# Values and the next pair's scores in one piece, and a new order of the last accumulators, in an attention and GLU kernel

## The chip, the cores and the metric

One of the eight NeuronCores of a Trainium2 chip runs the whole kernel. Its engines work from queues of their own and wait for each other through semaphores: TensorE (PE; its loads of weights are a row PEld), VectorE (DVE), ScalarE (ACT), GpSimd (POOL) and the queue engine SyncE (SP). The metric is device time in microseconds (us) of one execution.

## What is computed

Attention over 8 batches, 8 heads, 576 positions and 64 channels, with two kinds of sparse mask, and on its output a gated layer whose three products are with matrices of 512 x 1536, 512 x 1536 and 1536 x 512.

```python
def _attn_ref(q, k, v):
    scores = scale * np.matmul(q, k.transpose(0, 1, 3, 2))
    mask_local = (rel >= 0) & (rel < stride)              # stride = 32; heads 0 to 3
    mask_strided = (rel >= 0) & (pos[None, :] % stride == pos[:, None] % stride)   # heads 4 to 7
    ...
    attn = np.exp(scores - np.max(scores, axis=-1, keepdims=True))
    attn = attn / (np.sum(attn, axis=-1, keepdims=True) + 1e-09)
    return np.matmul(attn, v)

def _moe_ref(x, w_gate, w_val, w_out):     # x: 4608 tokens x 512
    gate = 1.0 / (1.0 + np.exp(-(x @ w_gate)))
    val = x @ w_val
    return gate * val @ w_out
```

## The kernel before

The gated layer goes over nine blocks of 512 tokens: block k holds the first 512 positions of batch k, and block 8 the 64 left over of all eight batches. A block has twelve chunks f of 128 hidden channels. Operands are kept as a high and a low part, and each product is made of three: high by high, low by high, high by low. So a chunk has three blocks of twelve TensorE products of 128 x 128 by 512: the gates g (`glu_gate`), the values v (`glu_val`), and the out-products o of a chunk (`glu_out`) into four accumulators of 128 tokens each. g and v have one PSUM bank each; the accumulators 0 and 1 share a tile of two banks, and 2 and 3 another; the last two banks are one tile "a" for attention.

Between the products stand the elementwise steps of a chunk. ScalarE makes t (tanh of half of g) and e (exp of g); VectorE clears t's sign (L386), multiplies min(e, 1) by v (L410), and by 1 + t (L411); ScalarE rounds it to hh (L402), VectorE makes hl, what is left (L405). t and e have one buffer each, hh and hl three.

Attention for batch k + 1 runs while block k does. A batch has four pairs of heads, local and strided in turn (`pair`), and a pair has these steps: Q and V load q with k, and v; Z clears pads; S makes the scores (small TensorE matmuls, `score`); F adds the mask, takes the maximum and subtracts it (VectorE); E is the exp (ScalarE); N the normalization (VectorE); B transposes the probabilities in 32 x 32 blocks (VectorE, L261); X weighs the values (small matmuls, `weigh`); H, L and R split the result into the high and low x of the coming block (xh on ScalarE, xl on VectorE), and keep the 64 positions left over (xr). Local scores use TensorE in tiles of 64 x 32, strided scores and all values in tiles of 64 x 64 (54 rows of it for strided values).

TensorE's order is written by hand: `block` walks the three slots of each chunk (gates, values, out-products of the chunk before), and calls the generator `attention` behind the slots 0 and 7 of every nine. Its first call of a pair records Q to B, its second X to R. So scores stand behind a chunk's gates, and the values of the same pair two chunks on, behind that chunk's values. The other engines' orders come from a scheduler. Batches 0 and 1 and block 0 are done in an earlier stage (`ORDER`) that the change leaves alone.

At a block's end `give_out` copies its four accumulators (ScalarE the even ones, VectorE the odd) and stores each through SP's queue. In block 8 the out-products of the last two chunks are done together, accumulator by accumulator; each is copied as soon as its products are done, the last one in two halves, one by each copying engine; and each copy is stored in two pieces of 64 rows, one for each batch. A read of a tile by a copy holds back later products into that tile.

Of the kernel before, what the change touches and what calls it, by code (L numbers as in the profile page):

```python
# [9 lines left out]
F32 = mybir.dt.float32  # L10
# [4 lines left out]
ALU = mybir.AluOpType  # L15
AX = mybir.AxisListType

B, H, S, D = 8, 8, 576, 64
DM, DF = 512, 1536
NT = B * S  # L20
P = 128
# [16 lines left out]
TB = 512  # L38
REST = S - TB
MAIN = TB // STRIDE  # L40
NTT = TB // P
NB = NT // TB
NC = DM // P
NF = DF // P
BANK = 512
BY_PE = 2
AT = (0, 7)
LATE = NF - 1

BANKS = {  # L50
# [33 lines left out]
def attention_then_glu(ctx, tc, qk_l, qk_s, v_l, v_s, w_all, consts, out):  # L84
    nc = tc.nc
    pool = ctx.enter_context(tc.tile_pool(name="keep", bufs=1))
    work = ctx.enter_context(tc.tile_pool(name="work", bufs=1))

    cst = pool.tile([P, SL * KL + GS + P], F32, name="cst")
    mask_l = cst[:, : SL * KL].rearrange("p (j n) -> p j n", j=1)  # L90
    mask_s = cst[:, SL * KL : SL * KL + GS].rearrange("p (t k) -> p t k", t=1)
# [3 lines left out]
    def left_over(b):  # L95

        if b == 0:
            xr[0] = pool.tile([P, NC, 2 * REST], F32, name="xr0")
        if b == 2:
            xr[2] = stage("raw1", "xr2").bitcast(F32).rearrange("p (c n) -> p c n", c=NC)  # L100
        if b == 6:
            xr[6] = stage("h0", "xr6").bitcast(F32).rearrange("p (c n) -> p c n", c=NC)
# [3 lines left out]
    def x_tiles(b):  # L106
        xs[b] = [(odd if b % 2 else work).tile([P, NC, TB], F32R, tag=t, name=f"{t}{b}") for t in ("xh", "xl")]
# [56 lines left out]
    def pair(b, step, space):  # L164

        local, p = step % 2 == 0, step // 2
        c = p if local else 2 + p
        ns, kk = (SL, KL) if local else (SS, GS)
# [26 lines left out]

        todo = {}

        def score(sc):
            qk = tiles["qk"]

            m = LB if local else QB
            for n in range(ns * (P // m)):
                s, g = divmod(n, P // m)
                q = n % (NBL if local else NG)
                for j in range(2):
                    d = slice(j * D, (j + 1) * D)
                    q0, k0 = (q * LB, S + q * LB) if local else (q * GS, SK + q * GS)
                    nc.tensor.matmul(  # L208
                        sc[g * m : (g + 1) * m, j * BANK + s * kk : j * BANK + (s + 1) * kk],
                        qk[d, q0 : q0 + m],  # L210
                        qk[d, k0 : k0 + kk],
                        start=True,
                        stop=True,
                    )
            todo["soft"] = sc.rearrange("p (j n) -> p j n", j=2)[:, :, : ns * kk]

        def soft():
            sc = todo["soft"]
            prob, row, by_row = rows()
            if local:  # L220
                to = tiles["sb"][:, : 2 * ns * kk].rearrange("p (j n) -> p j n", j=2)
                nc.vector.tensor_tensor(to, sc, mask_l.broadcast_to([P, 2, ns * kk]), op=ALU.add)
            else:
                for j in range(2):
                    to, sv = prob[:, j * ns : (j + 1) * ns], sc[:, j].rearrange("p (t k) -> p t k", k=kk)
                    nc.vector.tensor_tensor(to, sv, mask_s.broadcast_to([P, ns, kk]), op=ALU.add)
            nc.vector.tensor_reduce(row, prob, axis=AX.X, op=ALU.max)
            nc.vector.tensor_tensor(prob, prob, by_row, op=ALU.subtract)  # L228

# [96 lines left out]
        def keep_rest():  # L326
# [3 lines left out]

        return dict(
            Q=load_qk, V=load_v, Z=room, S=score, F=soft, E=expo, N=norm, T=turn, B=turn_blocks, P=spread, X=weigh, H=split_high,
            L=split_low, R=keep_rest,
        )

    def bank(tag, name):
        return ps.tile([P, 2 * BANK], F32, tag=tag, name=name)

    def attention(b):

        x_tiles(b)
        left_over(b)
        for step in range(4):
            do = pair(b, step, work)
            do["Q"](), do["V"](), do["Z"]()
            do["S"](bank("a", f"s{b}_{step}"))
            do["F"](), do["E"](), do["N"](), do["B"]()
            yield
            do["X"](bank("a", f"x{b}_{step}"))
            do["H"](), do["L"](), do["R"]()  # L350
            yield

    def split_rest():
# [17 lines left out]
    def glu_gate(k, f, g=None):  # L371
        if g is None:
            g = ps.tile([P, BANK], F32, tag="g", name=f"g{k}_{f}")
            products(g, k, f, 0)
        e = work.tile([P, TB], F32, tag="e", name=f"e{k}_{f}")
        hs[k, f] = e
        if k == 0:
            nc.scalar.activation(e, g, AF.Sigmoid)
            return
        t = work.tile([P, TB], F32, tag="t", name=f"t{k}_{f}")  # L380
        hs[k, f] = (t, e)

        nc.scalar.activation(t, g, AF.Tanh, scale=0.5)  # L383
        nc.scalar.activation(e, g, AF.Exp)  # L384
        ti = t.bitcast(I32)
        nc.vector.tensor_scalar(ti, ti, 0x7FFFFFFF, None, op0=ALU.bitwise_and)  # L386

    def glu_val(k, f, v=None):
        if v is None:
            v = ps.tile([P, BANK], F32, tag="v", name=f"v{k}_{f}")  # L390
            products(v, k, f, 1)
        if k == 0:
            e, t = hs[k, f], work.tile([P, TB], F32, tag="t", name=f"t{k}_{f}")
        else:
            t, e = hs[k, f]
        hh = work.tile([P, TB], F32R, tag="hh", name=f"hh{k}_{f}", bufs=3)
        hl = work.tile([P, TB], F32R, tag="hl", name=f"hl{k}_{f}", bufs=3)
        hs[k, f] = (hh, hl)
        half = 1.0 if k == 0 else 0.5

        def high():
            nc.scalar.activation(hh, t, AF.Copy, scale=half)  # L402

        def low():
            nc.vector.scalar_tensor_tensor(hl, t, half, hh.bitcast(F32), op0=ALU.mult, op1=ALU.subtract)  # L405

        if k == 0:
            nc.vector.tensor_tensor(t, e, v, op=ALU.mult)
            return high, low
        nc.vector.scalar_tensor_tensor(e, e, 1.0, v, op0=ALU.min, op1=ALU.mult)  # L410
        nc.vector.scalar_tensor_tensor(t, t, 1.0, e, op0=ALU.add, op1=ALU.mult)  # L411
        high(), low()
# [14 lines left out]
    def give_out(k, i, cut=slice(0, DM), by=None):  # L427

        tag = ("ost", "l0", "t", "e")[i if k == B else i % 2]
        if (k, i) not in given:  # L430
            given[k, i] = (odd if tag == "ost" else work).tile([P, DM], F32, tag=tag, name=f"ob{k}_{i}")
        ob, o = given[k, i], acc[k][i]
        if by is None:
            by = (nc.scalar.copy, nc.vector.tensor_copy)[i % 2]
        by(ob[:, cut], o[:, cut])  # L435
        if k < B:
            nc.sync.dma_start(out[k * S + i * P : k * S + (i + 1) * P, cut], ob[:, cut])
        else:
            for n in range(P // REST):
                at = (i * P // REST + n) * S + TB  # L440
                nc.sync.dma_start(out[at : at + REST, cut], ob[n * REST : (n + 1) * REST, cut])

    given = {}

    def glu_out(k, *fs):

        if fs[0] == 0:
            two = [bank(f"o{n}", f"o{k}_{n}") for n in range(NTT // 2)]
            acc[k] = [two[i // 2][:, i % 2 * BANK : (i % 2 + 1) * BANK] for i in range(NTT)]
        for i in range(NTT):  # L450
            for f in fs:
                out_products(k, f, i)
            if k == B and fs[-1] == NF - 1 and i < NTT - 1:
                give_out(k, i)
        if fs[-1] < NF - 1:
            return
        if k == B:
            give_out(k, NTT - 1, slice(0, DM // 2), nc.scalar.copy)
            give_out(k, NTT - 1, slice(DM // 2, DM), nc.vector.tensor_copy)
        else:  # L460
            for i in range(NTT):
                give_out(k, i)

    def block(k, f, pend, last):
        for slot in range(3):
            if slot == 0:
                glu_gate(k, f)
            elif slot == 1:
                glu_val(k, f)
            elif (k, f) != (B, NF - 2):  # L470
                glu_out(*last)
            if (3 * f + slot) % 9 in AT:
                next(pend, None)

    for f in range(LATE):
        weight_tiles(f)
# [54 lines left out]
                left_over(1)  # L531

    with tc.manual_schedule(engines={mybir.EngineType.PE}):
        last = (0, NF - 1)
        for k in range(1, NB):
            pend = attention(k + 1) if k + 1 < B else iter(())
            if k == B:
                split_rest()
            for f in range(NF):
                block(k, f, pend, last)  # L540
                last = (k, f) if (k, f) != (B, NF - 2) else last
            for _ in pend:
                pass
        glu_out(B, NF - 2, NF - 1)


# [81 lines left out]
```

## Time and profile before

| | |
|---|---|
| median of three runs | 1006.43 us (1006.33 to 1007.9) |
| the profiled execution, its own time | 1005.89 us |
| its span, first to last instruction | 1004.1 us |
| granted TensorE clock, mean | 0.996 |
| TensorE busy in the 540 us from 180 to 720 | 540.00 us |
| VectorE busy in the same stretch | 337.94 us |

A row of a timeline reads: start and length in us, engine, line of the kernel, operation, output <- inputs, shape, how many in the row, and in brackets how long the engine sat idle before it and what ended that. The chain of waits is followed back from the last instruction; its rows have a start, a length and what the time went to. An end of a matmul in the profile is a model; starts tell how fast TensorE goes.

### The profile page before, as it was taken

The page shows a single profiled execution, that of the slowest core. Times are in us where ns is not written, and L with a number is a line of the kernel's source. Part 1 is how long each engine was busy: PE and PEld are TensorE (multiplying, and loading weights), DVE is VectorE, ACT ScalarE, POOL GpSimd, SP SyncE. Part 2 cuts the span into 40 slices and gives each one's busy share as a digit, 9 for nine tenths or more (in the row PEclk, how much of TensorE's full clock was granted, in tenths as well). Part 3 has the DMA queues.
Part 4 walks back from the last instruction along what each step waited for, and adds up shares of the span by engine and source line. Part 5 has one row for each costly group of instructions (what it writes and reads, how often), then busy time and mean ns, then how long its engine had stood idle before and what let it go on. Part 6 is the DMA issues. An engine that isn't in the chain of part 4 may idle for free.

```text
span 1004.1 us, 18124 instructions
## 1 busy us (share of the span) xinstructions
PE 977.5 (97%) x7840; PEld 795.8 (79%) x7840; DVE 588.8 (59%) x1042; ACT 321.4 (32%) x636; POOL 5.1 (1%) x20
## 2 busy tenths in 40 slices
PE   4998999999999999999999999999999999999997
PEld 4787778888888888888888888888888888888885
DVE  6887776666666566656666666656665633333322
ACT  4787763222222222222322222222222322222221
POOL 0000000000000000000000000000000000000000
PEclk9999999999999999999999999999999999999999
DMA  7666641111211112101211121112110010001001
GB/s 249 225 178 202 207 122 68 41 52 41 90 44 52 41 57 78 40 29 51 84 28 49 41 93 41 52 41 73 61 52 17 1 43 1 0 1 42 1 1 42
DMA packets 20031, 66.02 MB, mean 66 GB/s; under 512 B 2288, under 2 KB 2672, under 8 KB 19952
## 3 DMA queue, kind: packets, MB, share of 16 engines
q1 hardware_dynamic: 18512, 59.28, 18.4%
q10 hardware_dynamic: 1440, 5.59, 1.6%
q8 instruction: 61, 1.00, 0.4%
q14 instruction: 18, 0.15, 0.0%
HBM read 55.42 MB, written 9.44 MB: 65 GB/s over the span
## 4 chain that ended last, share of the span: by engine, by line
PE 90%; DMA 4%; ACT 3%; DVE 2%; issue 0%; SPq 0%; ACTq 0%; DVEq 0%
PE v L369 28%; PE o L419 28%; PE g L369 27%; PE x L289 3%; DMA raw<-in_w_all 3%; PE s L208 3%; ACT high L139 1%; DMA qk<-in_qk_s 1%; ACT low L143 1%; PE t L247 1%; PE gv L369 1%; DVE sb L239 0%; DVE mx L236 0%; ACT sb L232 0%; ACT pt L269 0%
## 5 line engine op out<-in xcount | busy, mean ns | idle before, releaser
L419 PE MATMUL o<-w,hh 128*128 128x512 f32 x864 | 270.5, 394 | 1.4 <-ACT ob L435 1.4
L369 PE MATMUL v<-xh,w 128*128 128x512 f32 x784 | 263.3, 396 | 0.0
L369 PE MATMUL g<-xh,w 128*128 128x512 f32 x784 | 258.6, 390 | 0.0
L419 PEld LDWEIGHTS o<-w,hh 128*128 128x128 f32 x864 | 159.5, 188 | 37.3 <-ACT ob L435 2.2
L369 PEld LDWEIGHTS v<-xh,w 128*128 128x128 f32 x784 | 148.3, 189 | 32.8
L369 PEld LDWEIGHTS g<-xh,w 128*128 128x128 f32 x784 | 147.2, 188 | 30.9
L386 DVE TENSOR_SCALAR t<-t 128x512 int32<-128x512 int32 x96 | 41.0, 427 | 217.4 <-ACT t L383 216.6
L419 PE MATMUL o<-w,hl 128*128 128x512 f32 x432 | 168.4, 390 | 0.0
L369 PE MATMUL v<-xl,w 128*128 128x512 f32 x392 | 154.0, 393 | 0.0
L369 PE MATMUL g<-xl,w 128*128 128x512 f32 x392 | 152.7, 389 | 0.0
L402 ACT ACTIVATE hh<-t 128x512 fp32r<-128x512 f32 x108 | 68.3, 633 | 256.6 <-DVE t L411 256.0
L383 ACT ACTIVATE t<-g 128x512 f32<-128x512 f32 x96 | 57.4, 598 | 262.9 <-PE g L369 262.1
L410 DVE SCALAR_TENSOR_TENSOR e<-e,v 128x512 f32<-128x512 f32 x96 | 65.8, 686 | 91.0 <-PE v L369 91.0
L261 DVE STREAM_TRANSPOSE pt<-sb 32x320 f32<-32x320 f32 (+1 forms) x192 | 102.9, 536 | 3.1
L405 DVE SCALAR_TENSOR_TENSOR hl<-t,hh 128x512 fp32r<-128x512 f32 x108 | 74.6, 691 | 48.5 <-ACT hh L402 48.5
L419 PEld LDWEIGHTS o<-w,hl 128*128 128x128 f32 x432 | 81.1, 188 | 17.5 <-DVE hl L405 0.3
L369 PEld LDWEIGHTS v<-xl,w 128*128 128x128 f32 x392 | 74.3, 189 | 14.5
L369 PEld LDWEIGHTS g<-xl,w 128*128 128x128 f32 x392 | 73.6, 188 | 15.1
L411 DVE SCALAR_TENSOR_TENSOR t<-t,e 128x512 f32<-128x512 f32 x96 | 66.5, 692 | 3.3
L384 ACT ACTIVATE e<-g 128x512 f32<-128x512 f32 x96 | 57.0, 594 | 0.0
L232 ACT ACTIVATE sb<-sb 128x640 f32<-128x640 f32 (+1 forms) x32 | 23.8, 744 | 69.7 <-DVE sb L228 69.7
L289 PEld LDWEIGHTS x<-pt,vv 64*64 64x64 f32 (+1 forms) x1856 | 34.7, 140 | 13.8 <-issue 9.3
(60 smaller groups left out, 656.8 us busy)
## 6 DMA issues: line engine op xcount, KB each, us to landing
raw<-in_w_all SPq DMA_DIRECT2D x36, 512.0 KB, 4.2
qk<-in_qk_s SPq DMA_DIRECT2D x14, 599.0 KB, 4.2
vv<-in_v_l SPq DMA_DIRECT2D x13, 640.0 KB, 3.9
qk<-in_qk_l SPq DMA_DIRECT2D x14, 592.0 KB, 4.0
out<-ob SPq DMA_DIRECT2D x32, 256.0 KB, 2.0
vv<-in_v_s SPq DMA_DIRECT2D x13, 384.0 KB, 3.1
vv<-in_v_l ACTq DMA_DIRECT2D x3, 640.0 KB, 5.2
qk<-in_qk_s ACTq DMA_DIRECT2D x2, 599.0 KB, 4.4
```

The costliest lines, as they stand in the source:

```text
L208: nc.tensor.matmul(sc[g * m : (g + 1) * m, j * BANK + s * kk : j * BANK + (s + 1) * kk], qk[d, q0 : q0 + m], qk[d, k0 : k0 + kk], start=Tr ...
L261: nc.vector.transpose(dst[to : to + LB, :, col : col + LB], src[rows : rows + LB, :, h * LB : (h + 1) * LB])
L289: nc.tensor.matmul(xp[j * D : (j + 1) * D, r * BANK + (u * per + g) * m : r * BANK + (u * per + g + 1) * m], v[rows, (u * per + g) * P + j ...
L369: nc.tensor.matmul(o, w, x, start=first and n == 0, stop=last and n == len(todo) - 1)
L383: nc.scalar.activation(t, g, AF.Tanh, scale=0.5)
L384: nc.scalar.activation(e, g, AF.Exp)
L386: nc.vector.tensor_scalar(ti, ti, 0x7FFFFFFF, None, op0=ALU.bitwise_and)
L402: nc.scalar.activation(hh, t, AF.Copy, scale=half)
L405: nc.vector.scalar_tensor_tensor(hl, t, half, hh.bitcast(F32), op0=ALU.mult, op1=ALU.subtract)
L410: nc.vector.scalar_tensor_tensor(e, e, 1.0, v, op0=ALU.min, op1=ALU.mult)
L411: nc.vector.scalar_tensor_tensor(t, t, 1.0, e, op0=ALU.add, op1=ALU.mult)
L419: nc.tensor.matmul(acc[k][i], h[:, i * P : (i + 1) * P], w, start=f == 0 and n == 0, stop=f == NF - 1 and n == 2,)
```

## The change

A pair's values and the scores of the next pair are recorded by one call of the generator, which now runs over the 24 pairs of batches 2 to 7 without a break. The scores go into the g and v banks, one head in each, in place of tile "a"; only the very first pair's go into "a". Three chunks of a block with attention beside it have the order: gates and values of chunk 3n, out-products; gates and values of 3n + 1; gates and values of 3n + 2, out-products, the joined piece, out-products. Out-products so run one or two chunks behind. The load of a pair's v is recorded behind its F step, that of the next q and k at the end of the call. From block 7 on (no attention beside it) the order of the chunks is that of before.

Everywhere `glu_out` takes the accumulators in the order 0, 2, 1, 3. In block 8 each copy is stored by one DMA over two batches, from ScalarE's queue where ScalarE made the copy.

```diff
-AT = (0, 7)
...
-        def score(sc):
+        def score(*sc):
...
-                        sc[g * m : (g + 1) * m, j * BANK + s * kk : j * BANK + (s + 1) * kk],
+                        sc[j % len(sc)][g * m : (g + 1) * m, j // len(sc) * BANK + s * kk : j // len(sc) * BANK + (s + 1) * kk],
...
-                nc.vector.tensor_tensor(to, sc, mask_l.broadcast_to([P, 2, ns * kk]), op=ALU.add)
+                for j, x in enumerate(sc):
+                    heads = to[:, j : j + x.shape[1]]
+                    nc.vector.tensor_tensor(heads, x, mask_l.broadcast_to([P, x.shape[1], ns * kk]), op=ALU.add)
...
-    def attention(b):
-
-        x_tiles(b)
-        left_over(b)
-        for step in range(4):
-            do = pair(b, step, work)
-            do["Q"](), do["V"](), do["Z"]()
-            do["S"](bank("a", f"s{b}_{step}"))
-            do["F"](), do["E"](), do["N"](), do["B"]()
-            yield
-            do["X"](bank("a", f"x{b}_{step}"))
-            do["H"](), do["L"](), do["R"]()
+    def attention():
+
+        todo = [(b, step) for b in range(BY_PE, B) for step in range(4)]
+        ahead, now = pair(*todo[0], work), None
+        ahead["Q"]()
+        for n, (b, step) in enumerate(todo + [(B, 0)]):
+            if now:
+                of, p = todo[n - 1]
+                if p == 0:
+                    x_tiles(of)
+                    left_over(of)
+                now["X"](bank("a", f"x{of}_{p}"))
+                now["H"](), now["L"](), now["R"]()
+            if b < B:
+                now = ahead
+                now["Z"]()
+                if n == 0:
+                    now["S"](bank("a", f"s{b}_{step}"))
+                else:
+                    now["S"](*(ps.tile([P, BANK], F32, tag=t, name=f"s{b}_{step}_{t}") for t in "gv"))
+                now["F"](), now["V"](), now["E"](), now["N"](), now["B"]()
+                if n + 1 < len(todo):
+                    ahead = pair(*todo[n + 1], work)
+                    ahead["Q"]()
             yield
...
+        queue = nc.scalar if k == B and by == nc.scalar.copy else nc.sync
         if k < B:
-            nc.sync.dma_start(out[k * S + i * P : k * S + (i + 1) * P, cut], ob[:, cut])
+            to = out[k * S + i * P : k * S + (i + 1) * P, cut]
         else:
-            for n in range(P // REST):
-                at = (i * P // REST + n) * S + TB
-                nc.sync.dma_start(out[at : at + REST, cut], ob[n * REST : (n + 1) * REST, cut])
+            to = out.rearrange("(b s) n -> b s n", b=B)[i * P // REST : (i + 1) * P // REST, TB:, cut]
+        queue.dma_start(to, ob[:, cut])
...
-        for i in range(NTT):
+        for i in (0, 2, 1, 3):
...
             for f in range(NF):
-                block(k, f, pend, last)
-                last = (k, f) if (k, f) != (B, NF - 2) else last
-            for _ in pend:
-                pass
+                glu_gate(k, f)
+                glu_val(k, f)
+                last.append((k, f))
+                if k + 1 < B and f % 3 == 2:
+
+                    glu_out(*last.pop(0))
+                    next(pend)
+                    glu_out(*last.pop(0))
+                elif (k + 1 >= B or f % 3 == 0) and (k, f) != (B, NF - 2):
+                    glu_out(*last.pop(0))
+                if (k, f) == (1, 0):
+                    next(pend)
         glu_out(B, NF - 2, NF - 1)
```

Names in the rows below carry batch or block and pair or chunk: x2_1 are the weighted values of batch 2's pair 1, g1_6 the gates of block 1's chunk 6. xN at a row's end counts instructions.

TensorE in block 1, before: the values of pair 1 stand behind the products of chunk 5's values, and the scores of pair 2 behind chunk 6's gates.

```order
L369 MATMUL v1_5_2208<-xl1_570,w5_1_78 128x512
L369 MATMUL v1_5_2208<-xh1_569,w5_1_78 128x512
L289 MATMUL x2_1_2227<-pt2_1_2101,vv2_1_2062 64x54 x22
L419 MATMUL o1_0_1939<-w4_2_76,hh1_4_2172 128x512 x2
L419 MATMUL o1_0_1939<-w4_2_76,hl1_4_2173 128x512
...
L369 MATMUL g1_6_2271<-xl1_570,w6_0_80 128x512
L369 MATMUL g1_6_2271<-xh1_569,w6_0_80 128x512
L208 MATMUL s2_2_2295<-qk2_2_2289 32x64 x40
L369 MATMUL v1_6_2353<-xh1_569,w6_1_81 128x512
L369 MATMUL v1_6_2353<-xl1_570,w6_1_81 128x512
```

After, the same two stand next to each other, between the out-products of chunks 3 and 4:

```order
L433 MATMUL o1_1_1976<-w3_2_73,hh1_3_2126 128x512 x2
L433 MATMUL o1_1_1976<-w3_2_73,hl1_3_2127 128x512
L291 MATMUL x2_1_2230<-pt2_1_2072,vv2_1_2065 64x54 x22
L208 MATMUL s2_2_g_2264<-qk2_2_2081 32x64
L208 MATMUL s2_2_v_2265<-qk2_2_2081 32x64
```

The scores' 40 matmuls keep their order (the first two are shown), and go by turns into the g and the v bank; the products on both sides are out-products.

VectorE in block 2, from the mask add of a strided pair's scores on, before:

```order
L226 TENSOR_TENSOR sb3_3_3520<-s3_3_3523,cst_61 128x6x54 x2
L227 TENSOR_REDUCE mx3_3_3521<-sb3_3_3520 128x12
L228 TENSOR_TENSOR sb3_3_3520<-sb3_3_3520,mx3_3_3521 128x12x54
L410 SCALAR_TENSOR_TENSOR e2_9_3511<-e2_9_3511,v2_9_3566 128x512
L411 SCALAR_TENSOR_TENSOR t2_9_3512<-t2_9_3512,e2_9_3511 128x512
L236 TENSOR_REDUCE mx3_3_3521<-sb3_3_3520 128x12
L405 SCALAR_TENSOR_TENSOR hl2_9_3580<-t2_9_3512,hh2_9_3579 128x512
L237 TENSOR_SCALAR mx3_3_3521<-mx3_3_3521 128x12
L238 RECIPROCAL mx3_3_3521<-mx3_3_3521 128x12
L239 TENSOR_TENSOR sb3_3_3520<-sb3_3_3520,mx3_3_3521 128x12x54
L261 STREAM_TRANSPOSE pt3_3_3557<-sb3_3_3520 32x12x32 x8
L386 TENSOR_SCALAR t2_10_3611<-t2_10_3611 128x512
```

And after, from the same add on:

```order
L228 TENSOR_TENSOR sb3_3_3497<-s3_3_g_3500,cst_61 128x6x54
L228 TENSOR_TENSOR sb3_3_3497<-s3_3_v_3501,cst_61 128x6x54
L229 TENSOR_REDUCE mx3_3_3498<-sb3_3_3497 128x12
L230 TENSOR_TENSOR sb3_3_3497<-sb3_3_3497,mx3_3_3498 128x12x54
L238 TENSOR_REDUCE mx3_3_3498<-sb3_3_3497 128x12
L239 TENSOR_SCALAR mx3_3_3498<-mx3_3_3498 128x12
L240 RECIPROCAL mx3_3_3498<-mx3_3_3498 128x12
L241 TENSOR_TENSOR sb3_3_3497<-sb3_3_3497,mx3_3_3498 128x12x54
L263 STREAM_TRANSPOSE pt3_3_3537<-sb3_3_3497 32x12x32 x8
L400 TENSOR_SCALAR t2_9_3574<-t2_9_3574 128x512
L424 SCALAR_TENSOR_TENSOR e2_9_3573<-e2_9_3573,v2_9_3578 128x512
L425 SCALAR_TENSOR_TENSOR t2_9_3574<-t2_9_3574,e2_9_3573 128x512
```

The add of each head waits for its own bank; the instructions of chunk 9 (t, e, t, hl) stood between the pair's steps and stand behind all of them, the transposes too. At a change of block the copies of accumulators 1 and 3 stood on VectorE ahead of the normalization and behind the transposes; afterwards both stand behind the transposes, ahead of and behind the first chunk's hl.

The last rows of ScalarE and of SP's queue, before, ob8_n being the copy of accumulator n:

```order
L435 COPY ob8_0_8856<-o8_0_8358 128x512
L435 COPY ob8_2_8876<-o8_1_8359 128x512
L435 COPY ob8_3_8886<-o8_1_8359 128x256
L441 DMA out_0<-ob8_0_8856 64x512 x2
L441 DMA out_0<-ob8_1_8866 64x512 x2
L441 DMA out_0<-ob8_2_8876 64x512 x2
L441 DMA out_0<-ob8_3_8886 64x256 x4
```

And after:

```order
L449 COPY ob8_0_8890<-o8_0_8392 128x512
L455 DMA out_0<-ob8_0_8890 2x64x512
L449 COPY ob8_2_8899<-o8_1_8393 128x512
L455 DMA out_0<-ob8_2_8899 2x64x512
L449 COPY ob8_3_8917<-o8_1_8393 128x256
L455 DMA out_0<-ob8_3_8917 2x64x256
L455 DMA out_0<-ob8_1_8908 2x64x512
L455 DMA out_0<-ob8_3_8917 2x64x256
```

Ten stores on one queue become five, three on ScalarE's queue between its copies and two on SP's.

More of the change, by code (lines that the diff above doesn't have):

```diff
@@ L214, in score @@
                     )
-            todo["soft"] = sc.rearrange("p (j n) -> p j n", j=2)[:, :, : ns * kk]
+            todo["soft"] = [x.rearrange("p (j n) -> p j n", n=BANK)[:, :, : ns * kk] for x in sc]
         def soft():
@@ L221, in soft @@
                 to = tiles["sb"][:, : 2 * ns * kk].rearrange("p (j n) -> p j n", j=2)
-                nc.vector.tensor_tensor(to, sc, mask_l.broadcast_to([P, 2, ns * kk]), op=ALU.add)
+                for j, x in enumerate(sc):
+                    heads = to[:, j : j + x.shape[1]]
+                    nc.vector.tensor_tensor(heads, x, mask_l.broadcast_to([P, x.shape[1], ns * kk]), op=ALU.add)
             else:
                 for j in range(2):
-                    to, sv = prob[:, j * ns : (j + 1) * ns], sc[:, j].rearrange("p (t k) -> p t k", k=kk)
-                    nc.vector.tensor_tensor(to, sv, mask_s.broadcast_to([P, ns, kk]), op=ALU.add)
+                    sv = sc[j % len(sc)][:, j // len(sc)].rearrange("p (t k) -> p t k", k=kk)
+                    nc.vector.tensor_tensor(prob[:, j * ns : (j + 1) * ns], sv, mask_s.broadcast_to([P, ns, kk]), op=ALU.add)
             nc.vector.tensor_reduce(row, prob, axis=AX.X, op=ALU.max)
@@ L462, in glu_out @@
                 give_out(k, i)
[L464 to L473, printed above, removed]
     for f in range(LATE):
@@ L533, in attention_then_glu @@
     with tc.manual_schedule(engines={mybir.EngineType.PE}):
-        last = (0, NF - 1)
+        last = [(0, NF - 1)]
+        pend = attention()
         for k in range(1, NB):
-            pend = attention(k + 1) if k + 1 < B else iter(())
             if k == B:
```

## The prediction

> **What bounds the kernel now.** First the page: its busy times and its chain.
>
> ```profile
> PE 977.5 (97%) x7840; PEld 795.8 (79%) x7840; DVE 588.8 (59%) x1042; ACT 321.4 (32%) x636; POOL 5.1 (1%) x20
> PE 90%; DMA 4%; ACT 3%; DVE 2%; issue 0%; SPq 0%; ACTq 0%; DVEq 0%
> ```
>
> TensorE is busy for 97% of the span and holds 90% of the chain. An edit pays only if it shortens TensorE's stream itself, a wait inside it, or what comes after its last product. Second the chain of waits, in order of time, in an undisturbed stretch: one block of 12 products of 512 columns takes 2.72 us, back to back.
>
> ```profile
> 187.53 2.72 PE g L369 x12
> 190.25 2.72 PE v L369 x12
> ```
>
> Third the timeline of TensorE around the pieces of attention (s are scores, x are weighted values; xN counts the profile's matmuls, two for each float32 instruction).
>
> ```profile
> 180.63 0.39 PE L369 MATMUL g<-xh,w 128*128 128x512 f32 x1
> 180.94 0.92 PE L208 MATMUL s<-qk 64*64 64x54 f32 x48
> 181.79 0.50 PE L369 MATMUL v<-xh,w 128*128 128x512 f32 x1
> ...
> 200.74 0.39 PE L369 MATMUL v<-xh,w 128*128 128x512 f32 x1
> 201.06 0.91 PE L289 MATMUL x<-pt,vv 54*64 54x54 f32 x44
> 201.90 0.73 PE L419 MATMUL o<-w,hh 128*128 128x512 f32 x2
> ...
> 204.75 0.39 PE L369 MATMUL g<-xh,w 128*128 128x512 f32 x1
> ...
> 207.56 1.04 PE L208 MATMUL s<-qk 64*32 64x64 f32 x80
> 208.53 0.50 PE L369 MATMUL v<-xh,w 128*128 128x512 f32 x1
> ...
> 227.83 1.35 PE L289 MATMUL x<-pt,vv 64*64 64x32 f32 x72
> 229.12 0.73 PE L419 MATMUL o<-w,hh 128*128 128x512 f32 x2
> ...
> 235.63 0.50 PE L369 MATMUL v<-xh,w 128*128 128x512 f32 x1
> ```
>
> From 181.79 to 235.63 lie 18 blocks and four pieces, one of each kind: 53.84 us. The blocks alone are 18 x 2.72 = 48.96. The pieces, from their first matmul to the first product behind them, are 0.97 + 0.84 + 1.29 + 0.85 = 3.95. So 53.84 - 48.96 - 3.95 = 0.93 us is neither: it is paid at the four pieces' borders, 0.23 each. Its two halves can be seen. **In**: a product starts 2.72/12 = 0.227 after the one ahead of it, but the piece of 180.94 starts 0.31 behind its last product, so 0.09 too much. **Out**: the block behind the piece of 201.06 takes 204.75 - 201.90 = 2.85, so 0.13 too much.
>
> **The change part by part.** *Pieces in one.* Six batches of four pairs make 24 score pieces and 24 value pieces, 48 in all; afterwards there is one score piece, 23 joined ones and one value piece, 25. Each joint drops the out of the values (0.13) and the in of the scores (0.09). The matmuls stay the same in number, shape and array position; only the PSUM banks of the scores differ. So 23 x 0.22 = 5.1 us, if the joint costs nothing of its own. No row of before shows values followed by scores. The nearest are scores followed by values, in the start stage, on the row of weight loads (and the loads of one later piece):
>
> ```profile
> 16.50 1.16 PEld L208 LDWEIGHTS s<-qk 64*32 64x32 f32 x80 [1.07 <-ACT pt L271]
> 17.84 2.34 PEld L289 LDWEIGHTS x<-pt,vv 64*64 64x64 f32 x72 [0.17 <-issue]
> ...
> 22.73 1.37 PEld L208 LDWEIGHTS s<-qk 64*64 64x64 f32 x48 [1.35 <-ACT pt L269]
> 23.97 1.41 PEld L289 LDWEIGHTS x<-pt,vv 54*64 54x64 f32 x44
> ...
> 180.94 0.79 PEld L208 LDWEIGHTS s<-qk 64*64 64x64 f32 x48 [0.35 <-issue]
> ```
>
> With different tiles (64x32, then 64x64) the loads pause 0.17; with equal ones they don't. Twelve joints are values to strided scores (equal tiles), eleven values to local scores (64x64, then 64x32). In these rows everything small runs slower than later (80 score matmuls take 17.84 - 16.50 = 1.34, later 0.97), and the 0.84 to 1.29 of a value piece contains the drain at its end already. Bounds for a joint: dearest, 0.17 at all 23, leaves 23 x 0.05 = 1.2; cheapest, a joint that also spares that drain at twelve, 0.06 each (the loads of 180.94 end at 181.73, the next product starts at 181.79), is 5.8. I take 5.1, nearest to the rows with equal tiles.
>
> The Trainium skill bears on this: "TensorEngine Tiling (Array Packing)", section Tiling Modes, says that a change of tiling mode, not merely of tile, drains TensorE. That speaks against eleven of the joints; priced at the pause above it would take 11 x 0.17 = 1.9 off, a total of 7.7 in place of the 9.6 below. The four rows agree with it in kind; for values followed by scores no run here shows it.
>
> *The wait at a block's first accumulators.* The waits and the chain:
>
> ```profile
> PEld o L419 <- DVE ob L435: 2.0, 6, 0.3
> 273.58 2.95 PE o L419 x12
> 276.53 2.75 PE g L369 x12
> ```
>
> Six times the first out-products of a block wait for VectorE's copy of the last accumulator, which stood behind a pair's transposes: (2.95 - 2.72) + (2.75 - 2.72) = 0.26, so 1.5 us. Before, two blocks (gates, values; 5.4 us) lie between the last out-products and the next first ones; now four (10.9 us). The last copy still stands behind the transposes and the first chunk's instructions, yet has twice the time. The wait goes: 1.5, bounds 0 and 1.6.
>
> *The end.* The chain in its last window, and the stores:
>
> ```profile
> 988.82 4.09 PE o L419 x18
> 992.93 0.59 ACT ob L435
> 993.57 3.03 PE o L419 x12
> 997.26 1.68 PE o L419 x6
> 998.96 0.38 ACT ob L435
> 999.37 0.42 DVE ob L435
> ...
> L441 SPq DMA_DIRECT2D out<-ob x10: 467/563/593, 993.5 to 1001.2; - x10
> ...
> out<-ob SPq DMA_DIRECT2D x6, 128.0 KB, 2.3
> out<-ob SPq DMA_DIRECT2D x4, 64.0 KB, 2.0
> ```
>
> Accumulators 0 and 1 share a PSUM tile, as do 2 and 3; products of 1 wait for the copy of 0, and of 3 for that of 2. In the order 0, 2, 1, 3 a copy of 0.59 has the 6 products of the other tile (1.36) to hide under. TensorE then ends at 992.91 + 18 x 0.227 = 997.0 in place of 997.26 + 1.68 = 998.94: 1.94 earlier. ScalarE's half copy and VectorE's half behind it stay as they are, so VectorE ends at 999.79 - 1.94 = 997.85 and its one store is issued there. Before, the last of four stores of 64 rows is issued at 1001.2, behind the queue's earlier ones. The last issue comes 3.3 earlier. What one store of 2x64 rows costs is not in the trace: an issue between 0.47 (the cheapest of 64 rows) and twice 0.56, a landing between 2.0 and 2.3. That gives 3.4 to 2.4; I take 3.0 (one 0.56, landing 2.3). The other stores of these halves go out from ScalarE's queue ahead of its next copy: its issues of some 0.6 fit in the 1.36 between two accumulators.
>
> *Two chunks in a row.* A block of values directly behind the next gates has 2.72 where it had 5.44 in which VectorE must have read the old values, and VectorE now does a pair's whole softmax and its transposes in one run, ahead of the chunk's own four instructions. Rows of one such run (three instructions of a chunk are mixed into it, e and hl shown and t between them, of the same size; they now stand behind it):
>
> ```profile
> 182.08 0.89 DVE L226 TENSOR_TENSOR sb<-s,cst 128x324 f32<-128x324 f32 x2
> 184.92 0.69 DVE L410 SCALAR_TENSOR_TENSOR e<-e,v 128x512 f32<-128x512 f32 x1 [0.21 <-PE v L369]
> 187.03 0.69 DVE L405 SCALAR_TENSOR_TENSOR hl<-t,hh 128x512 fp32r<-128x512 f32 x1
> 193.99 0.68 DVE L410 SCALAR_TENSOR_TENSOR e<-e,v 128x512 f32<-128x512 f32 x1
> 196.10 0.69 DVE L405 SCALAR_TENSOR_TENSOR hl<-t,hh 128x512 fp32r<-128x512 f32 x1 [0.70 <-ACT hh L402]
> 190.29 0.60 ACT L383 ACTIVATE t<-g 128x512 f32<-128x512 f32 x1 [3.29 <-PE g L369]
> 190.78 0.59 ACT L384 ACTIVATE e<-g 128x512 f32<-128x512 f32 x1
> ```
>
> Count from the end of a joined piece. The mask add starts by 1.0 (the split of the values ahead of it is short) and takes 0.89, so the gates' bank is free by 1.9, against 2.85 at which the next gates start (one block of out-products lies between). The values of that chunk are read at 1.0 + (194.67 - 182.08) - 3 x 0.69 = 11.5; the bank is wanted at 2.85 + 4 x 2.72 = 13.7: **2.2 to spare**. The chunk's hl is done at 1.0 + (196.79 - 182.08) - 2.07 = 13.6; the next chunk's tanh and exp (190.29 to 191.37, 1.08) wait for it and for gates that end at 13.7, so they are done by 14.9, and the second gates in a row want the bank at 16.45: **1.5 to spare**. At a change of block two copies of accumulators (0.69 each) stand on VectorE as well, one of them ahead of hl: 0.8 to spare. I cost this part at nothing. Should the cover be gone, every 0.1 us beyond it costs 24 x 0.1 = 2.4. On SP's queue the loads of a pair's values and of the next q and k alternate as before, each behind the piece that frees its buffer; both now wait for the same joined piece and have about a pair's nine blocks until use. POOL's clearing of a strided pair's pads goes with the scores and waits for the same transposes.
>
> Sum: 5.1 + 1.5 + 3.0 = **9.6 us**. The profiled run took 1005.89 (span 1004.1), so 996.3 there; the median of the runs, 1006.43, stands 0.5 above it, so **996.8**.
>
> **The rivals.** *A: the joint costs as much as it saves.* For it: the 0.17 pause; against it: equal tiles pass without a pause. Then 1.5 + 3.0 = 4.5 remains, 1001.9; with half of the saving 999.4. *B: VectorE's run becomes the bound (slower).* Place: second gates or values in a row, once in each of the 24 pairs. It decides from 1.5 us of delay (0.8 at a change of block), and from 1.5 + 9.6/24 = 1.9 on the kernel is slower than before. A delay of 2.5, say, would cost 24 x 1.0 = 24 us: 996.8 + 24 = 1020.8. For it: the run is unbroken for some 11 us; against it: VectorE is busy for 59% only and each figure in the count is a row's. *C: it isn't one piece.* The scores wait for VectorE's read of the values and the exp of the gates; if they come late, in and out are paid as before and a wait besides: 1002 to 1006. Against it: both reads have a block of out-products (2.72) and the value piece as cover. *D: the store of 2x64 rows is dear*, two issues' worth and more: 1 us, 997.8.
>
> **How the numbers follow.** Forecast (with D) 0.74, from 994.9 (5.8 + 1.6 + 3.4 = 10.8 and 0.7 for the spread between runs) to 999; A 0.14; C 0.05; B 0.07. The range runs from 994.5 to 1002, through A. A measurement of this kernel can tell 0.2%, 2 us, from no change: faster by more holds for the forecast, A and most of C; 0.91. Within it: the dear end of C and the start of B, 0.03. Slower: 0.06.
>
> **What would show it.** In the changed trace values and scores should follow each other with no product between, the pause between their weight loads telling the joint's price; blocks of 2.72 everywhere else; one pair's time 9 x 2.72 plus one piece and one border, some 26.7 for the mean of the two kinds, in place of 53.84 / 2 = 26.92. No wait of out-products for VectorE at a block's first chunk. At the end no gap between the 24 last products, and one store issue behind VectorE's half copy. I am wrong if gates or values wait for ScalarE or VectorE between the pieces, or if the second block after a piece starts late.

## The result and the profile after

| | before | after |
|---|---|---|
| median | 1006.43 us | 1010.8 us |
| lowest and highest of 14 runs | 1002.4 to 1010.33 | 1008.05 to 1016.82 |
| the profiled execution, its own time | 1005.89 | 1008.05 |
| its span | 1004.1 | 1005.9 |
| VectorE's last half copy ends | 999.79 | 985.63 |
| from there to the end of the span | 4.31 | 20.27 |

The changed kernel is slower: ratio 1.0054 of the time before, 95% interval 1.0034 to 1.0074, which is 3.4 to 7.4 us. The forecast was 996.8 with a range of 994.5 to 1002, so it missed. The last two rows of the table already say where. VectorE's last half copy ends 14.16 us earlier than before, and the end of the span does not follow it: some 20 us pass in which no engine computes. (3.55 of the 14.16 lie in the start stage, as shown below.)

The page of the changed kernel, busy times and shares of the chain, and the last pieces of its chain of waits (start, length, what):

```profile
PE 966.6 (96%) x7840; PEld 796.0 (79%) x7840; DVE 596.8 (59%) x1053; ACT 323.9 (32%) x636; POOL 6.7 (1%) x20
PE 90%; DMA 3%; DVE 2%; ACT 2%; issue 0%; SPq 0%; ACTq 0%; DVEq 0%
```

```profile
976.51 8.28 PE o L433 x36
...
984.81 0.38 ACT ob L449
985.19 0.02 issue
985.21 0.42 DVE ob L449
```

TensorE's busy time has fallen from 977.5 to 966.6. Of these 10.9 us 1.7 lie in the start stage (133.54 to 131.82), and the rest, 9.2, is near the 8.5 that the forecast asked of TensorE (5.1 + 1.5 + 1.94). The 36 last matmuls take 8.28 us with hardly a gap (36 x 0.227 = 8.17). But the chain's last computing piece ends at 985.63 in a span of 1005.9. What fills the rest is in the windows of the changed kernel's end (length; busy time and count of PE, PEld, DVE, ACT, POOL; granted clock; mean busy share of the 16 DMA engines; GB/s):

```profile
985.00:990.00 5.00, 0.00 (x0) 0.00 (x0) 0.42 (x1) 0.18 (x1) 0.00 (x0) 0.99 0.13 48
990.00:995.00 5.00, 0.00 (x0) 0.00 (x0) 0.00 (x0) 0.00 (x0) 0.00 (x0) 0.50 0.13 52
995.00:1000.00 5.00, 0.00 (x0) 0.00 (x0) 0.00 (x0) 0.00 (x0) 0.00 (x0) 0.50 0.13 50
1000.00:1005.90 5.90, 0.00 (x0) 0.00 (x0) 0.00 (x0) 0.00 (x0) 0.00 (x0) 0.50 0.11 39
```

The same view of the end before:

```profile
990.00:995.00 5.00, 4.33 (x19) 3.28 (x18) 1.03 (x2) 1.22 (x2) 0.00 (x0) 1.00 0.05 12
995.00:1000.00 5.00, 3.25 (x13) 2.01 (x12) 1.11 (x2) 0.96 (x2) 0.00 (x0) 1.00 0.65 145
1000.00:1004.10 4.10, 0.00 (x0) 0.00 (x0) 0.00 (x0) 0.00 (x0) 0.00 (x0) 0.95 0.27 64
```

Both ends store the same 1 MB. Before, the DMA engines were busy for 0.65 on the mean and moved 145 GB/s. After, the share stands at 0.13 for 15 us, and 0.13 x 16 = 2.1: two engines of sixteen work all the time, and move some 50 GB/s. The records of single packets in the same trace agree: from 987 to 1000 two packets are under way at once, and three for a tenth of the time, where before, from 995 to 1000, there are up to 17. The packets of data have 1 or 2 KB in both. 1.05 MB at 50 GB/s is 21 us. SP's queue waits for exactly these stores at the program's end (row of the waits of SP: total, times, longest):

```profile
SPq L635 <- DMA out<-ob: 18.7, 2, 18.2
```

The issues themselves are in the timeline of the changed kernel (ACTq and SPq rows are stores put on a queue):

```profile
980.62 0.59 ACT L449 COPY ob<-o 128x512 f32<-128x512 f32 x1 [1.93 <-PE o L433]
981.24 1.14 ACTq L455 DMA_DIRECT2D out<-ob  x1
...
983.10 0.53 ACTq L455 DMA_DIRECT2D out<-ob  x1
...
984.12 2.08 SPq L455 DMA_DIRECT2D out<-ob  x2
...
985.21 1.99 ACTq L455 DMA_DIRECT2D out<-ob  x1
```

The five issues begin between 981.24 and 985.66, in the places that were forecast. The longest takes 1.99 us, and the last, at 985.66, takes 0.53. Not the issue is dear but the transfer.

To compare kernels, two marks cut each span in three: T, the start of ScalarE's first tanh (t) of block 1, and A, the start of its copy of accumulator 0 in block 8 (980.62 above). T ends the start stage, whose code the change leaves alone.

| us | T | T to A | A to end | span |
|---|---|---|---|---|
| before | 153.59 | 839.34 | 11.17 | 1004.1 |
| after | 150.04 | 830.58 | 25.28 | 1005.9 |
| difference | -3.55 | -8.76 | +14.11 | +1.8 |

So the change by itself makes -8.76 + 14.11 = +5.35, inside the measured interval. T differs between executions of the same start code (from 149.37 to 155.07 in the nine profiled executions of this study), and that is left out of every comparison below that is made by the trace.

### The profile page after: what moved, and what is told of

Read it like the earlier page. It is cut to its first block, busy times and chain, and to the rows that moved or that the text cites. A ratio compares the mean times of both kernels' runs of the same rounds, so it can differ in the third digit from the quotient of the medians.

```text
span 1005.9 us, 18068 instructions
## 1 busy us (share of the span) xinstructions
PE 966.6 (96%) x7840; PEld 796.0 (79%) x7840; DVE 596.8 (59%) x1053; ACT 323.9 (32%) x636; POOL 6.7 (1%) x20
## 4 chain that ended last, share of the span: by engine, by line
PE 90%; DMA 3%; DVE 2%; ACT 2%; issue 0%; SPq 0%; ACTq 0%; DVEq 0%
PE o L433 28%; PE v L383 28%; PE g L383 27%; PE x L291 3%; DMA raw<-in_w_all 2%; PE s_v L208 1%; PE s_g L208 1%; PE s L208 1%; DMA qk<-in_qk_l 1%; DMA qk<-in_qk_s 1%; PE gv L383 1%; ACT high L138 1%; ACT low L142 0%; PE t L249 0%; DVE w L161 0%
## 5 line engine op out<-in xcount | busy, mean ns | idle before, releaser
L383 PE MATMUL v<-xh,w 128*128 128x512 f32 x784 | 259.2, 391 | 0.0
L383 PEld LDWEIGHTS g<-xl,w 128*128 128x128 f32 x392 | 73.6, 188 | 15.1
L326 DVE TENSOR_TENSOR xl<-x,xh 128x512 fp32r<-128x512 f32 (+1 forms) x64 | 24.2, 420 | 38.8 <-ACT xh L322 38.8
```

Source lines behind the costliest of these rows:

```text
L383: nc.tensor.matmul(o, w, x, start=first and n == 0, stop=last and n == len(todo) - 1)
```

## The experiments

The theory: a store of 2x64 rows goes to only two DMA engines, because its outermost count is 2. Two rivals: Q, the stores are slow since they now go out from ScalarE's queue; S, they are slow since one transfer spans two batches that lie far apart in the output. Beside them the other terms are measured alone: the joined pieces, and the order of the accumulators.

| | runs | median, us | ratio to before (95%) | T to A | A to end |
|---|---|---|---|---|---|
| e1_two_stores | 6 | 993.43 | 0.9885 (0.9855 to 0.9915) | 830.58 | 8.62 |
| e2_before_one_store | 4 | 1019.48 | 1.015 (1.0114 to 1.0187) | 839.32 | 25.17 |
| e3_one_store_first | 6 | 998.56 | 0.9927 (0.9902 to 0.9952) | 830.59 | 11.74 |
| e4_one_store_last | 6 | 998.34 | 0.9938 (0.9913 to 0.9963) | 830.58 | 13.75 |
| e5_order_only | 12 | 1006.8 | 1.0013 (0.9994 to 1.0031) | 843.57 | 9.46 |
| e6_rows_of_62 | 10 | 1011.81 | 1.0048 (1.003 to 1.0067) | 830.58 | 25.41 |
| e7_join_only | 6 | 997.35 | 0.9897 (0.9877 to 0.9917) | 830.59 | 11.14 |

The ratio is to runs of the kernel before that were taken alongside (median 1004.36 for e1 to e4, 1006.52 for e5 to e7); it is not simply the quotient of the medians.

### e1: the changed kernel with two stores of 64 rows

Nothing but the one store is taken back; order and queues stay.

```diff
-            to = out.rearrange("(b s) n -> b s n", b=B)[i * P // REST : (i + 1) * P // REST, TB:, cut]
+            for n in range(P // REST):
+                at = (i * P // REST + n) * S + TB
+                queue.dma_start(out[at : at + REST, cut], ob[n * REST : (n + 1) * REST, cut])
+            return
```

> The changed kernel, but each copy of block 8 is stored by two DMAs of 64 rows, one for each batch, on the queue on which the change has its one store. Theory P (a store over two batches of 64 rows runs on two of the 16 DMA engines, and five of them queue up there): the span ends about 2.9 us after the last store's issue, as before, instead of 20.2; so 17.3 less than the changed kernel's 1010.8, about 993.5, and 12 to 13 below the kernel before. Rival Q (ScalarE's queue is what is slow, its issues took 0.5 to 2.0 us): still some 20 us after the last issue, 1010. Rival R (the loss is in the joined pieces): 1010 too.

993.43 us: faster than both kernels, by 10.9 than the one before, where 12 to 13 were expected. A to end falls from 25.28 to 8.62, 16.7 us, with T to A unchanged. Windows of its end, and its DMA issues (KB each, median us from issue to landing):

```profile
980.00:985.00 5.00, 5.00 (x23) 3.92 (x23) 0.87 (x2) 1.18 (x2) 0.00 (x0) 1.00 0.23 52
985.00:990.00 5.00, 0.58 (x3) 0.14 (x1) 0.42 (x1) 0.37 (x1) 0.00 (x0) 0.78 0.60 157
```

```profile
out<-ob ACTq DMA_DIRECT2D x4, 128.0 KB, 2.3
out<-ob SPq DMA_DIRECT2D x2, 128.0 KB, 2.4
out<-ob ACTq DMA_DIRECT2D x2, 64.0 KB, 2.2
out<-ob SPq DMA_DIRECT2D x2, 64.0 KB, 2.0
```

The same bytes from the same two queues land 2.0 to 2.4 us behind their issue, at a DMA share of 0.60. ScalarE's queue isn't slow, and the joined pieces are the same as in the changed kernel: rivals Q and R fall.

### e2: the kernel before with one store of 2x64 rows

The reverse: all of before, and only the store of the change, on SP's queue.

```diff
-            for n in range(P // REST):
-                at = (i * P // REST + n) * S + TB
-                nc.sync.dma_start(out[at : at + REST, cut], ob[n * REST : (n + 1) * REST, cut])
+            to = out.rearrange("(b s) n -> b s n", b=B)[i * P // REST : (i + 1) * P // REST, TB:, cut]
+            nc.sync.dma_start(to, ob[:, cut])
```

> The kernel before with one change: each copy of block 8 is stored by one DMA of 2x64 rows, all on SP's queue, the order of the accumulators as before. Theory P: the changed kernel's stores took from 981.2 to 1005.9, 24.7 us for 1 MB; here the first is issued at 993.5, so the end comes near 1018 in place of 1004.1, 13 to 14 us slower than before. Rival Q: nothing goes out from ScalarE's queue, so no loss, and up to 1 us faster by the issues saved. Rival R: no change.

15.1 us slower than before by the medians, 14.0 by A to end. Windows of its end:

```profile
1005.00:1010.00 5.00, 0.00 (x0) 0.00 (x0) 0.00 (x0) 0.00 (x0) 0.00 (x0) 0.50 0.13 51
1010.00:1018.00 8.00, 0.00 (x0) 0.00 (x0) 0.00 (x0) 0.00 (x0) 0.00 (x0) 0.50 0.12 45
```

Share and rate are those of the changed kernel though every store goes out from SP. The store alone is enough to make a loss of this kind.

### e6: pieces of 62 rows inside one batch

Each copy is stored as 62 and 2 rows of each of the two batches, so no store spans two batches; 62, like 2, has no divisor up to 16 but 1 and 2.

```diff
-            to = out.rearrange("(b s) n -> b s n", b=B)[i * P // REST : (i + 1) * P // REST, TB:, cut]
+            for n in range(P // REST):
+                at = (i * P // REST + n) * S + TB
+                for lo, hi in ((0, REST - 2), (REST - 2, REST)):
+                    queue.dma_start(out[at + lo : at + hi, cut], ob[n * REST + lo : n * REST + hi, cut])
+            return
```

> As the run with two stores for each copy, but each of them is cut into one of 62 rows and one of 2 rows, every one inside one batch. Theory P in its sharper form (the number of DMA engines is the largest one up to 16 that divides the outermost count of both sides, 2 for 62 as for 2x64): all on two DMA engines again, a DMA share of 0.13 at the end, 25 us or more from ScalarE's first copy to the span's end, about 1011 to 1014. Rival S (it is the two batches, 1.2 MB apart, in one store that is slow): as with two stores, 8.6 us from the first copy and 994, plus up to 2 us for the issues of ten more stores.

1011.81, as slow as the changed kernel; A to end 25.41 against its 25.28. Windows of its end:

```profile
990.00:995.00 5.00, 0.00 (x0) 0.00 (x0) 0.42 (x1) 0.37 (x1) 0.00 (x0) 0.50 0.13 51
995.00:1000.00 5.00, 0.00 (x0) 0.00 (x0) 0.00 (x0) 0.00 (x0) 0.00 (x0) 0.50 0.13 50
```

Rows of a single batch, the same share of 0.13 and the same 50 GB/s: rival S falls. Between 64 rows (e1) and 62 and 2 rows lies the whole loss. One caution: e6 has twice as many stores as e1, and eight of them take SP's queue 15.04 us to issue; ScalarE's last copy waits 6.99 us for such stores and comes only after 990. That the engines stay at 0.13 of their time is the reading that decides.

The Trainium skill, "DMA: Bandwidth & Descriptors", section "Why a DMA increments its semaphore by 16 and not by 1", has the rule that fits: a DMA is dealt out over the largest number of engines, up to 16, that divides the outermost count on both of its sides. By it 64 rows go to 16 engines, and 62 rows or 2 batches to two. The shares agree: 0.13 for the last two, and 0.60 for the first, which two engines can't reach.

### e4 and e3: one store of 2x64 rows only for the last, or only for the first accumulator

e4 has two stores of 64 rows for the accumulators 0, 1 and 2, and keeps the 2x64 rows for both halves of 3:

```diff
+            if i < 3:
+                for n in range(P // REST):
+                    at = (i * P // REST + n) * S + TB
+                    queue.dma_start(out[at : at + REST, cut], ob[n * REST : (n + 1) * REST, cut])
+                return
```

> As the run with two stores, but the two halves of accumulator 3, the last to be copied, are stored by one DMA of 2x64 rows each, from ScalarE's and SP's queue. Theory P: 256 KB on the same two DMA engines, 6.2 us from the first half's issue, 0.4 us ahead of the last; so the end comes about 6 in place of 2.9 us after the last issue: 3 us above the run with two stores. If each queue had two DMA engines of its own, 3.1 + 1: about 1 us above.

A to end is 13.75, 5.1 over e1: a miss by 2 us. Windows of its end:

```profile
985.00:987.00 2.00, 0.00 (x0) 0.00 (x0) 0.42 (x1) 0.37 (x1) 0.00 (x0) 1.00 0.77 204
987.00:990.00 3.00, 0.00 (x0) 0.00 (x0) 0.00 (x0) 0.00 (x0) 0.00 (x0) 1.00 0.13 37
990.00:993.00 3.00, 0.00 (x0) 0.00 (x0) 0.00 (x0) 0.00 (x0) 0.00 (x0) 0.53 0.13 48
```

256 KB are left for two engines; at 50 GB/s they take 5.2 us, here from about 987 to 993. I had put these 5.2 in the place of a store's landing of 2.0 to 2.4 us; but the transfer begins over a microsecond behind the issue (985.87 for the last one), and the span ends 1.5 behind it, so they come on top. The cause stands; the estimate lacked a term. That each queue has two engines of its own, about 1 us, falls.

e3 has the condition `if i > 0:` in place of `if i < 3:`. One 2x64 store of 256 KB is put out first, 3.5 us ahead of the end of the products (985.77, they end by 989.3), and so was to be hidden.

> As the run with two stores, but accumulator 0, the first to be copied, is stored by one DMA of 2x64 rows. Theory P: 256 KB on two DMA engines take a quarter of 24.7, 6.2 us, from some 7 us ahead of the usual end: hidden, the time of the run with two stores within 1 us. A fixed cost of such a store of 10 us or more, not one by its bytes, would show as 4 us or more.

It isn't: A to end is 11.74, 3.1 over e1. (The medians differ by 5.1, but T is 154.57 in the one profile and 150.80 in the other, in code that both share.) DMA issues of e3, and three windows of its end:

```profile
out<-ob ACTq DMA_DIRECT2D x2, 128.0 KB, 6.7
out<-ob SPq DMA_DIRECT2D x2, 128.0 KB, 5.5
out<-ob ACTq DMA_DIRECT2D x2, 64.0 KB, 5.4
out<-ob SPq DMA_DIRECT2D x2, 64.0 KB, 4.8
```

```profile
987.00:988.00 1.00, 1.00 (x6) 0.69 (x5) 0.07 (x1) 0.59 (x1) 0.00 (x0) 1.00 0.12 29
...
993.00:994.00 1.00, 0.00 (x0) 0.00 (x0) 0.00 (x0) 0.00 (x0) 0.00 (x0) 0.50 0.20 74
994.00:995.00 1.00, 0.00 (x0) 0.00 (x0) 0.00 (x0) 0.00 (x0) 0.00 (x0) 0.50 0.13 47
```

The later stores of 64 rows, whose like landed after 2.0 to 2.4 us in e1, take 4.8 to 6.7. One slow store delays all behind it, on both queues; I had taken them as independent of it. This fits if each later store has a share on the two engines that still move the first, and lands with its slowest share. An estimate: those two engines have the 256 KB of the first store, 128 KB each, and a sixteenth of the other 768 KB, 48 KB each; 176 KB at 25 GB/s (half of the 50 above) take 7.2 us, from 987 to about 994. The windows agree: when the other engines are done, two are busy until 995. That they are the same two is argued, since the trace doesn't name the engine of a packet. A fixed cost of 10 us for such a store isn't needed: in e4 two of them, 256 KB in all, took about 6 us, near the 5.2 of their bytes.

### e7: the joined pieces without the new end

The changed kernel with the stores, the queue and the order of before.

```diff
-        queue = nc.scalar if k == B and by == nc.scalar.copy else nc.sync
+        queue = nc.sync
...
-            to = out.rearrange("(b s) n -> b s n", b=B)[i * P // REST : (i + 1) * P // REST, TB:, cut]
+            for n in range(P // REST):
+                at = (i * P // REST + n) * S + TB
+                queue.dma_start(out[at : at + REST, cut], ob[n * REST : (n + 1) * REST, cut])
+            return
...
-        for i in (0, 2, 1, 3):
+        for i in range(NTT):
```

> The changed kernel with the end of before: accumulators in the order 0 to 3, two stores of 64 rows for each copy, all on SP's queue. If the joined pieces and the vanished wait at a block's first accumulators are worth what the trace of the changed kernel says (10.6 us from block 1's first gates to the last product, 1.9 of it the order), 8.7 less than the kernel before: 0.9914 of its time, near 996. If they are worth what was forecast, 6.6: 0.9934. If the gain seen there was the start stage's luck, 1.000.

The ratio is 0.9897; its interval holds the first of the three figures, 0.9914, and not the other two. T to A is 830.59: 8.75 us less than before, and to 0.01 us that of the changed kernel. A to end, 11.14, is that of before (11.17). So pieces and end are independent here, and all that the trace of after gains before A comes from the pieces and the wait that went with them.

### e5: the kernel before with the order 0, 2, 1, 3 alone

```diff
-        for i in range(NTT):
+        for i in (0, 2, 1, 3):
```

> The kernel before with the accumulators in the order 0, 2, 1, 3 and nothing else: the two waits of TensorE for ScalarE's copies near the end go, 0.95 us each, and the stores stay as they were. From ScalarE's copy of accumulator 0 to the span's end: 11.2 us before, 9.2 here. About 2 us less than the kernel before, 0.998 of its time, which five rounds may not tell from the spread of the start stage; the trace does. If the waits had another cause, 11.2 stays.

No gain in sum: 1.0013. A to end does fall by 1.71 (11.17 to 9.46), but T to A grows by 4.23: 2.5 more by the trace, inside the interval, which ends at 3.1 us. Waits of TensorE in e5 (total, times, longest), and its chain at the change from block 1 to block 2:

```profile
PEld o L419 <- DVE ob L435: 6.5, 6, 1.1
PE o L419 <- DVE ob L435: 4.0, 6, 0.7
```

```profile
267.36 2.73 PE v L369 x12
...
270.15 0.51 DVE pt L261
...
270.68 0.70 DVE ob L435
...
271.43 2.33 PE o L419 x9
273.76 2.72 PE g L369 x12
```

The order holds for every `glu_out`, not only for the last. At a block's start it makes the products of accumulator 2 the second group, three products in, and these need the tile that accumulators 2 and 3 share. VectorE's copy of 3 out of it stands behind the transposes (pt). From the end of the values (267.36 + 2.73 = 270.09) to 273.76 it is 3.67 in place of 2.72, so 0.95 is lost. Before, those products came third, and the wait cost 0.26 per block: 0.69 more now, and 6 x 0.69 = 4.1 is nearly all of the 4.23 measured. In the changed kernel the same order costs nothing (T to A of after and of e7 are the same): four blocks lie there in front of these products, not two, and at the same change of block VectorE's last copy ends at 267.55, 6.3 us ahead of the out-products at 273.82.

## Why the prediction was wrong

**The step that failed** is the third term, the end: "What one store of 2x64 rows costs is not in the trace". The text bounded it by an issue of 0.47 to 1.12 and a landing of 2.0 to 2.3, taken from stores of 64 rows, and expected the end 3.0 earlier. It came 14.1 later. The bound was drawn around the wrong quantity: it let the issue double and kept the landing, that is, it took for granted that a store uses all DMA engines whatever the shape of its pattern. e1 and e2 put a price on the step from both sides: 25.28 - 8.62 = 16.7 us in the new schedule, 25.17 - 11.17 = 14.0 in the old one. The issue was bounded rightly: the last one, at 985.66, took 0.53. It was the transfer, which ran on two engines at 50 GB/s in place of all sixteen. Rival D, "the store of 2x64 rows is dear", had the right place, and 1 us for it.

What the trace of before could have raised as a question: its last stores are 1 MB, and move at 145 GB/s in a window with a DMA share of 0.65. A store on fewer engines would then be the first thing to fear at an end with nothing behind it to hide it. With the rule of the Trainium skill cited at e6, two engines for 2x64 rows would have been the forecast; the prediction drew on another page and had no such rival.

**The joint** was right in kind and too small: T to A is 8.75 shorter in e7, less the 1.5 of the wait 7.25, or 0.31 for each of the 23 joints in place of 0.22 (5.1 in all). Rows of TensorE in the changed kernel, first a strided pair's values with local scores, then a local pair's values with strided scores, and the out-products behind each:

```profile
597.91 0.73 PE L433 MATMUL o<-w,hh 128*128 128x512 f32 x2
...
622.62 0.91 PE L291 MATMUL x<-pt,vv 54*64 54x54 f32 x44
...
624.42 0.73 PE L433 MATMUL o<-w,hh 128*128 128x512 f32 x2
...
649.12 1.29 PE L291 MATMUL x<-pt,vv 64*64 64x32 f32 x69
...
651.13 0.73 PE L433 MATMUL o<-w,hh 128*128 128x512 f32 x2
```

Two pairs now take 651.13 - 597.91 = 53.22 in place of 53.84, so 0.31 per joint here too. The piece with equal tiles takes 2.01, while its parts took 1.29 + 0.85 = 2.14 apart: it saves 0.13 inside as well. The one with different tiles takes 1.80, against 0.84 + 0.97 = 1.81. The prediction had allowed 0.06 for the first, and only as its cheap end. Twelve times 0.13 + 0.22 and eleven times 0.01 + 0.22 make 6.7 of the 7.25. Most of the rest is an out that is dearer than the 0.13 of the prediction: before, the block of values behind a local pair's scores took 2.89 (208.53 to 211.42), and the out-products behind the same scores in their joined piece take 2.85 (624.42 to 627.27). That is 0.04 for each of the eleven, 0.4 in all.

The change of tiles, which the Trainium skill spoke against, is on the row of weight loads of the same piece:

```profile
622.62 0.78 PEld L291 LDWEIGHTS x<-pt,vv 54*64 54x64 f32 x44 [0.35 <-issue]
623.45 0.10 PEld L208 LDWEIGHTS s_g<-qk 64*32 64x32 f32 x1
```

The pause is 623.45 - 623.40 = 0.05, not 0.17, and the piece is no longer than its parts. The rule of the Trainium skill ("TensorEngine Tiling (Array Packing)", section Tiling Modes), that a change of mode drains TensorE, isn't contradicted: equal tiles do save the 0.13 that these don't. But a drain, if there is one, was paid before too, at the border to the products, and takes nothing off; no run here shows the drain itself.

**The wait at a block's first accumulators** went, as forecast: of the row with 2.0 us for VectorE nothing is left; among the waits of weight loads for a copy the one row quoted below remains, 0.2 us for ScalarE. Its price shows in the distance from one local pair's values to the next: before, they start at 173.99, 227.83, 281.93, 335.76 and 389.86, 53.84 apart inside a block and 54.10 over a change of block; in the changed kernel at 170.20, 223.42, 276.63 and 329.84, about 53.21 apart each time. So 0.26 went at each of six changes, the 1.5 of the forecast. **The cover of two chunks in a row** held. The stretch from 180 to 720 of the changed kernel, VectorE's wait for the values, and the chain where the values' bank (665.02) and the second gates in a row (667.74) are wanted behind the joined piece of 649.12:

```profile
180.00:720.00 540.00, 540.00 (x4636) 446.47 (x4636) 351.19 (x621) 144.28 (x293) 4.80 (x10) 1.00 0.16 53
```

```profile
PEld o L433 <- ACT ob L449: 0.2, 1, 0.2
...
DVE e L424 <- PE v L383: 108.8, 72, 1.7
```

```profile
665.02 2.72 PE v L383 x12
667.74 2.72 PE g L383 x12
670.46 2.72 PE v L383 x12
```

TensorE is busy for all of the 540 us, but it was so before too, with the waits of 1.5 us inside, so that alone proves nothing. What counts is that it is VectorE that waits for values, 72 times, that no wait of a product for VectorE is left between the pieces, and that these blocks start on time and take their 2.72. So rivals B and C have no support in the trace, and the 0.31 of a joint rules out A.

**The order at the end** was forecast to bring 1.94 of the 3.0. e5 shows 1.71 for it alone. e1, which has ScalarE's queue besides, has an end of 8.62, so 9.46 - 8.62 = 0.84 more; together that is 2.55, the gain at the end without the slow store. What the prediction didn't say is that the order acts at every block; it was free only because the schedule was changed at the same time (e5).

In sum, by the trace: forecast 6.6 + 3.0 = 9.6 earlier; measured 8.76 earlier and 14.11 later. With the stores of 64 rows (e1) it is 8.76 + 2.55 = 11.3, and the medians of that session say 1004.36 - 993.43 = 10.9. The version to keep is e1.

## What to carry to other kernels

Merging several stores into one can lower the number of DMA engines that move it: ask of each new pattern how its outermost count divides before asking what the issue costs, and see that no such transfer stands at an end with nothing to hide it, nor ahead of others. In windows of the profile its mark was a DMA share that stayed at 0.13, two sixteenths, while nothing else ran. An order that is chosen for one place should be looked at in every place that shares the code.

## What was unexpected of the hardware

- Stores of 2x64 rows, of 62 and of 2 rows kept the DMA engines at 0.13 of their time, two of 16, at 50 GB/s; stores of 64 rows (e1) reached 157 GB/s at 0.60 in the mean of the last window.
- Two engines at 50 GB/s move 25 each; sixteen at a share of 0.60 and 157 GB/s move 157 / (0.60 x 16) = 16 each while busy.
- Stores of 64 rows that were issued behind one of 2x64 rows landed after 4.8 to 6.7 us in place of 2.0 to 2.4 (e3), also from the other queue.
- Small matmuls in equal tiles that follow each other directly take 0.13 us less than in two pieces with products between, beside what the borders to the products cost.
